# Computing the first W1 piece of batch 1 in the same array-mode group as batch 0's second piece

## The chip, the cores and the metric

One core of one Trainium2 chip. The metric is device time of one execution in microseconds (us); lower is better. Most executions agree within 0.3%, which is 0.6 us here, and the change is worth less than that, so much of this document is about how to see 0.2 us at all.

## The reference

Eight batches of cross attention between a sequence and a small state, both ways, then a two-layer block with silu over all the rows:

```python
scores = scale * x @ state.T ;  a  = softmax(scores)  ; xread = a  @ state   # (8, 8, 512, 64)
scores2 = scale * state @ x.T;  a2 = softmax(scores2) ; sread = a2 @ x       # (8, 8, 32, 64)
rows = concat([xread, sread], axis=2), heads joined                          # (4352, 512)
h = rows @ w_in                      # (., 2048)
out = (h * sigmoid(h)) @ w_out       # (., 512)
```

## The kernel before

The product `state @ w_in` is made once for each batch and called W1, so that `xread @ w_in` is `a @ W1`. W1 is 2048 columns wide and is made in pieces of 512. "G1 of tile k" is one 128-column tile of `a @ W1` (two matmuls) followed by silu on ScalarE; "G2 of tile k" is that tile's part of the last product (four matmuls for the four row groups of a batch).

A piece of W1 contracts over 64 and has 32 rows a head, so it uses the matmul array as eight tiles of 64x32. Eight matmuls, one a tile, make a piece into two PSUM banks. PSUM is the memory that the matmuls write their results to; a copy from there to the working memory (SBUF) is called an eviction below. The kernel uses eight PSUM banks: `psA` a0 to a3, `psH` two (tag h1), `psO` two.

```python
# cut: setup lines, returns and some arguments are left out; the whole kernel is below
def w1_mms(b, cols, new=bank):              # eight matmuls in 64x32 tiles
    for f, n in cols:
        for hg in range(2):
            pss[f, hg] = new([128, 512], FP32, "ps_w1")
        for s in range(4):
            for hg in range(2):
                nc.tensor.matmul(pss[f, hg][ds(32 * s, 32), 0:n], stT[ds(r, 64), b, ...],
                                 w_in_sb[ds(r, 64), h // 2, ds(f, n)], tile_position=(r, 32 * s), ...)
def w1_out(b, cols, engs, pss, at=0):       # PSUM to SBUF, one bank by VectorE, one by ScalarE
    ...
def g1_half(k, hg):
    if hg == 0:
        pool, tag = (psA, "a1") if k == 1 else (psH, "h1")
        h_ps[k] = pool.tile([128, 512], FP32, tag=tag, name="h1")
    nc.tensor.matmul(h_ps[k][:], W1[b][:, hg, ds(128 * ft, 128)], aT[b][:, hg, :, :], ...)

# loads on the GpSimd queue, in order (cut)
load_w_in(0, 128); load_w_in(128, 384); load_w_out(0, 2); load_w_out(2, 2)
# ... state of batch 1 ...
load_w_in(512)
load_w_out(4, 4)          # output weights of tiles 4 to 7, one transfer
# ... GpSimd's part of the first cast of x, normalisation ...
load_w_in(1024)
load_w_out(8, 4)

# batch 0
W0 = {2: (512, 512), 6: (1024, 512), 10: (1536, 512)}    # pieces of batch 0, by step
W1_AT = {4: 0, 6: 512}                                   # pieces of batch 1
LEAD0 = [2, 2, 2, 2, 2, 3, 2, 1, 3, 3, 2, 3]
for ft in range(12):
    upto(min(ft + LEAD0[ft], ready))                     # G1 of the next tiles
    if ft == 1:
        place_one_state(1, transpose_one_state(st1_n), nc.vector)
    if ft in W0:
        pss = w1_mms(0, [W0[ft]])
        if ft in W1_AT:
            pss1 = w1_mms(1, [(W1_AT[ft], 512)], new_h)  # rides in the same group
        w1_out(0, [W0[ft]], both, pss)
        if ft in W1_AT:
            w1_out(1, [(W1_AT[ft], 512)], both, pss1)
        ready = sum(W0[ft]) // 128
    elif ft in W1_AT:
        w1_cols(1, [(W1_AT[ft], 512)], both)             # a group of its own
    # ... G2 of tile ft ...
```

The softmax here doesn't subtract the row's maximum and nothing guards it: scores larger than these inputs give would overflow.

## Time and profile before

| | before |
|---|---|
| median of the first three runs | 213.09 us (213.04 to 213.17) |
| the profiled run | 214.55 us, span of the trace 212.8 us |
| matmul engine busy | 97% |
| ScalarE, VectorE, GpSimd busy | 65%, 35%, 19% |

The matmul groups of the page (line engine op, out<-in, shapes, count | busy us, mean ns of one | idle before; in these views PE is the matmul engine, PEld its weight loads, ACT is ScalarE, DVE VectorE and POOL GpSimd):

```profile
L563 PE MATMUL o<-w_out_sb,g 128*128 128x512 bf16 x481 | 129.5, 379 | 1.3 <-issue 0.5
L522 PE MATMUL h<-aT,W 128*128 128x512 bf16 x247 | 73.1, 379 | 0.2
L468 PE MATMUL ps_w<-w_in_sb,stT 64*32 64x512 bf16 (+2 forms) x264 | 10.2, 374 | 0.0
```

A matmul's 379 ns is its recorded length; they overlap and start 216 ns apart. The W1 groups (L468) are 264 of the 1550 matmuls recorded but only 10.2 us, since eight run together; what they cost beyond that are the holes at their edges.

### The profile page before, as it was taken

The page shows a single profiled execution, that of the slowest core. Times are in us where ns is not written, and L with a number is a line of the kernel's source. Part 1 is how long each engine was busy: PE and PEld are TensorE (multiplying, and loading weights), DVE is VectorE, ACT ScalarE, POOL GpSimd, SP SyncE. Part 2 cuts the span into 40 slices and gives each one's busy share as a digit, 9 for nine tenths or more (in the row PEclk, how much of TensorE's full clock was granted, in tenths as well). Part 3 has the DMA queues.
Part 4 walks back from the last instruction along what each step waited for, and adds up shares of the span by engine and source line. Part 5 has one row for each costly group of instructions (what it writes and reads, how often), then busy time and mean ns, then how long its engine had stood idle before and what let it go on. Part 6 is the DMA issues. An engine that isn't in the chain of part 4 may idle for free.

```text
span 212.8 us, 3839 instructions
## 1 busy us (share of the span) xinstructions
PE 205.8 (97%) x1550; PEld 97.9 (46%) x1575; DVE 73.8 (35%) x146; ACT 139.1 (65%) x244; POOL 39.9 (19%) x62
## 2 busy tenths in 40 slices
PE   7899999999999999999999999999999999999993
PEld 2543445345444434444444444444444444466653
DVE  2672246855851137104410752143512306100011
ACT  2685667899676877699469856886775256644410
POOL 8393213702420122012200302000200000000000
PEclk9999999999999999999999999999999999999998
DMA  5999999995639567464826429114230121011112
GB/s 189 192 205 207 285 261 313 249 242 203 99 78 265 174 130 170 101 195 102 218 64 211 79 53 240 49 52 99 65 83 17 64 82 52 0 49 49 52 49 99
DMA packets 42929, 28.65 MB, mean 135 GB/s; under 512 B 28064, under 2 KB 37792, under 8 KB 42912
## 3 DMA queue, kind: packets, MB, share of 16 engines
q1 hardware_dynamic: 36720, 20.65, 36.3%
q0 software_dynamic: 5904, 7.64, 17.4%
q8 instruction: 12, 0.20, 0.4%
q10 hardware_dynamic: 288, 0.13, 0.2%
q14 instruction: 5, 0.04, 0.1%
HBM read 17.43 MB, written 8.91 MB: 124 GB/s over the span
## 4 chain that ended last, share of the span: by engine, by line
PE 94%; DMA 2%; DVE 1%; issue 1%; ACT 0%
PE o L563 50%; PE h L522 26%; PE ps_w L468 4%; PE h L543 3%; PE o_a L563 3%; DMA x_f<-in_x_dram 2%; PE o_part L585 2%; PE ps_xt L252 1%; PE ps_sr L415 1%; PE ps_busy L165 1%; PE ps_sc L305 1%; PE ps_scT L331 1%; DVE W L159 1%; PE ps_at L397 0%; ACT xT L157 0%
## 5 line engine op out<-in xcount | busy, mean ns | idle before, releaser
L563 PE MATMUL o<-w_out_sb,g 128*128 128x512 bf16 x481 | 129.5, 379 | 1.3 <-issue 0.5
L554 ACT ACTIVATE g<-h 128x512 bf16<-128x512 f32 (+1 forms) x143 | 81.3, 573 | 35.3 <-PE h L522 20.6
L563 PEld LDWEIGHTS <-g 128*128 128x128 bf16 x528 | 50.2, 98 | 58.9 <-issue 3.8
L522 PE MATMUL h<-aT,W 128*128 128x512 bf16 x247 | 73.1, 379 | 0.2
L159 DVE COPY o_sb<-o 128x512 f32<-128x512 f32 x15 | 10.4, 690 | 91.9 <-PE o L563 87.3
L522 PEld LDWEIGHTS <-W 128*128 128x128 bf16 x254 | 24.4, 98 | 30.7 <-issue 1.2
L159 DVE CAST W<-ps_w 128x512 bf16<-128x512 f32 (+2 forms) x36 | 22.3, 658 | 23.8 <-PE ps_w L468 23.8
L157 ACT ACTIVATE W<-ps_w 128x512 bf16<-128x512 f32 (+1 forms) x32 | 16.3, 562 | 10.2 <-PE ps_w L468 10.2
L159 POOL CAST x_nat<-x_f 128x512 bf16<-128x512 f32 x24 | 14.6, 648 | 33.2 <-DMA x_f<-in_x_dram 33.2
L157 ACT ACTIVATE o_sb<-o 128x512 f32<-128x512 f32 x16 | 9.5, 597 | 14.3 <-PE o L563 11.8
L361 POOL TENSOR_TENSOR an<-e,rcn 128x512 bf16<-128x512 bf16 x5 | 7.6, 1517 | 49.1 <-DVE rcn L359 49.1
L468 PE MATMUL ps_w<-w_in_sb,stT 64*32 64x512 bf16 (+2 forms) x264 | 10.2, 374 | 0.0
L543 PE MATMUL h<-xmT,w_in_sb 128*128 128x256 bf16 x64 | 9.6, 273 | 0.1
L563 PE MATMUL o_a<-w_out_sb,g 128*128 128x512 bf16 x30 | 9.4, 379 | 0.1
L543 PEld LDWEIGHTS <-w_in_sb 128*128 128x128 bf16 x64 | 6.3, 98 | 3.9
L165 PE MATMUL ps_busy<-busy 128*128 128x512 bf16 x15 | 6.8, 563 | 1.2 <-DVE warm L172 1.2
L358 DVE TENSOR_REDUCE rs<-e 128x32 f32<-128x1024 bf16 x5 | 6.1, 1210 | 2.1 <-DMA e<-eT 2.1
L345 ACT ACTIVATE eT<-ps_scT 128x512 bf16<-128x512 f32 x10 | 5.4, 594 | 1.6 <-PE ps_scT L331 1.6
L784 ACT ACT_TABLE_LOAD x5 | 6.4, 1283 | 0.1
L381 POOL TENSOR_TENSOR an<-exp_nat,rc 128x512 bf16<-128x512 bf16 x3 | 3.1, 1046 | 17.7 <-ACT eT L345 10.8
L468 PEld LDWEIGHTS <-stT 64*32 64x32 bf16 x264 | 3.2, 90 | 5.5 <-issue 4.7
L109 POOL DMA_DIRECT2D x_f<-in_x_dram x4 | 3.3, 845 | 10.2 <-DVE x_rows L159 7.9
(76 smaller groups left out, 103.7 us busy)
## 6 DMA issues: line engine op xcount, KB each, us to landing
out_dram<-o_sb SPq DMA_DIRECT2D x33, 256.0 KB, 2.4
x_f<-in_x_dram SPq DMA_DIRECT2D x4, 1024.0 KB, 5.8
x_f<-in_x_dram POOLq DMA_DIRECT2D x2, 1024.0 KB, 11.1
w_in_sb<-in_moe_w_in_dram POOLq DMA_DIRECT2D x3, 512.0 KB, 10.1
x_f<-in_x_dram SPq DMA_DIRECT2D x2, 512.0 KB, 5.2
w_out_sb<-in_moe_w_out_dram POOLq DMA_DIRECT2D x4, 256.0 KB, 11.4
w_out_sb<-in_moe_w_out_dram POOLq DMA_DIRECT2D x2, 512.0 KB, 11.2
x_f<-in_x_dram POOLq DMA_DIRECT2D x2, 512.0 KB, 13.5
```

The lines of the kernel that those rows point to most:

```text
L157: nc.scalar.activation(dst, src, func=COPY, bias=0.0)
L159: eng.tensor_copy(dst, src)
L165: nc.tensor.matmul(ps[:], busy[:, 0:128], busy[:], start=True, stop=True, skip_group_check=True)
L345: nc.scalar.activation(t[:, hg], scT_ps[hg][:], func=EXP, bias=0.0, scale=SCALE)
L358: nc.vector.tensor_reduce(rs[:], e2[b][:], axis=AX, op=ADD)
L361: eng.tensor_tensor(a[:, hg], e2[b][:, hg], rc[:, hg].to_broadcast([128, 4, 4, NS]), op=MULT)
L468: nc.tensor.matmul(pss[f, hg][ds(32 * s, 32), 0:n], stT[ds(r, 64), b, h // 2, s % 2, :], w_in_sb[ds(r, 64), h // 2, ds(f, n)], start=True, ...
L522: nc.tensor.matmul(h_ps[k][:], W1[b][:, hg, ds(128 * ft, 128)], aT[b][:, hg, :, :], start=(hg == 0), stop=(hg == 1), skip_group_check=True,)
L543: nc.tensor.matmul(ps[:, 0:256], w_in_sb[:, kt, ds(128 * ft, 128)], xmT[:, :, kt].rearrange("p t n b -> p t (n b)"), start=(kt == 0), stop ...
L554: nc.scalar.activation(g[:, 0:n], ps[:, 0:n], func=SILU, bias=0.0)
L563: nc.tensor.matmul(outs[tt][:], gt[b * NFT + ft][:, ds(128 * tt, 128)], w_out_sb[:, ft, :], start=(ft == 0), stop=(ft == NFT - 1), skip_gr ...
L784: nc.scalar.activation(warm[:], busy[:, 0:1], func=SILU, bias=0.0)
```

## The change

Intent: each time the array changes between its full mode and the tiled one there is a hole in the stream of matmuls. Batch 0's second piece (step 2) and batch 1's first piece (step 4) were two groups. Now the latter rides in the group of step 2, in the two `psH` banks. Those banks must be free, so G1 of tile 3 goes one step earlier (`LEAD0[1]`), and while they are full G1 of tiles 4 and 5 goes to the two banks of batch 0's piece.

```diff
     def g1_half(k, hg):
         if hg == 0:
-            pool, tag = (psA, "a1") if k == 1 else (psH, "h1")
-            h_ps[k] = pool.tile([128, 512], FP32, tag=tag, name="h1")
+            if k == 1:
+                h_ps[k] = psA.tile([128, 512], FP32, tag="a1", name="h1")
+            else:
+                h_ps[k] = (bank if k in IN_BANKS else new_h)([128, 512], FP32, "h1")
...
+    IN_BANKS = (4, 5)
...
-    W1_AT = {4: 0, 6: 512}
-    LEAD0 = [2, 2, 2, 2, 2, 3, 2, 1, 3, 3, 2, 3]
+    W1_AT = {2: 0, 6: 512}
+    LEAD0 = [2, 3, 2, 2, 2, 3, 2, 1, 3, 3, 2, 3]
...
-        elif ft in W1_AT:
-            w1_cols(1, [(W1_AT[ft], 512)], both)
```

## The prediction

> **What bounds the kernel now.** I read the page first: busy shares, then the chain that ended last, then the instructions in order of time around the changed stage.
>
> ```profile
> PE 205.8 (97%) x1550; PEld 97.9 (46%) x1575; DVE 73.8 (35%) x146; ACT 139.1 (65%) x244; POOL 39.9 (19%) x62
> PEclk9999999999999999999999999999999999999998
> ...
> PE 94%; DMA 2%; DVE 1%; issue 1%; ACT 0%
> ```
>
> The matmul engine is busy for 97% of 212.8 us, its clock is never throttled, and it is 94% of the chain. No other engine is above 65%. So time comes off only if the stream of matmuls has fewer of them, or fewer gaps. The list of waits shows what gaps there are (engine and line <- releaser: us in total, times, longest):
>
> ```profile
> PEld L468 <- issue: 4.7, 12, 0.4
> PEld L563 <- issue: 3.8, 10, 0.4
> ```
>
> L468 is the W1 product, made of 64x32 tiles of the array; L563 is a full 128x128 product. Each of the twelve runs of L468 has a 0.4 us hole in the weight loads ahead of it, put down to no wait for another engine, and most have another behind. The changed stage in order of time (start, length, engine, line, tiles, count):
>
> ```profile
> 14.92 0.22 PE L206 MATMUL ps_st<-ident,st_n 128*128 128x128 bf16 x1
> 14.98 0.59 PE L563 MATMUL o<-w_out_sb,g 128*128 128x512 bf16 x2
> 15.41 0.81 PE L563 MATMUL o_a<-w_out_sb,g 128*128 128x512 bf16 x3
> 16.06 0.59 PE L522 MATMUL h<-aT,W 128*128 128x512 bf16 x2
> 16.58 0.41 PE L468 MATMUL ps_w<-w_in_sb,stT 64*32 64x512 bf16 x8
> 16.92 0.39 PE L563 MATMUL o<-w_out_sb,g 128*128 128x512 bf16 x1
> ...
> 19.11 0.59 PE L522 MATMUL h<-aT,W 128*128 128x512 bf16 x2
> 19.63 0.11 PEld L468 LDWEIGHTS <-stT 64*32 64x32 bf16 x8 [0.42 <-issue]
> 19.97 0.55 PEld L563 LDWEIGHTS <-g 128*128 128x128 bf16 x4 [0.23 <-issue]
> ...
> 22.14 0.59 PE L563 MATMUL o_a<-w_out_sb,g 128*128 128x512 bf16 x2
> 22.67 0.63 PE L468 MATMUL ps_w<-w_in_sb,stT 64*32 64x512 bf16 x16
> 23.23 0.60 PE L563 MATMUL o<-w_out_sb,g 128*128 128x512 bf16 x2
> ```
>
> A group of 8 at 16.58 (second piece of batch 0), another of 8 at 19.64 (first piece of batch 1), a group of 16 at 22.67 (a piece of each). The change makes the first two one group of 16, at the place of the first. The rest of the span repeats what the third shows.
>
> **What the Trainium skill says.** "TensorEngine Tiling (Array Packing)", Key Properties: "Changing tiling mode (not just tile) drains the TensorE". The trace agrees in effect: full-array matmuls follow one another at 0.216 us (15.409, 15.625, 15.840 by the recorded starts), but the group starts 0.309 after the matmul before it (16.272 to 16.581), and the next full one 0.318 after the group's last start (16.605 to 16.923).
> "TensorE: Matmul & The Clock Gate", The mechanism: different tiles run together, about 4 ns apart. Here the eight starts run from 16.581 to 16.605, 3.4 ns apart, and the second eight of the group of 16 begin 0.203 us after the last of the first eight (22.694 to 22.897). So a set of eight costs about one full matmul.
> "PSUM — Partial Sum Buffer", PSUM bank collisions: the semaphores must guard whole banks. That is why the riding piece needs banks of its own, and why the two G1 results must go elsewhere. No collision is in question here.
>
> **The change part by part.** The order of instructions of the changed kernel against the old one on each engine (built, not run) shows equal counts on every engine, no change of order on VectorE, GpSimd and the DMA queue, one ScalarE eviction moved two places up, and the matmul order restored after G1 of tile 5. So nothing is computed less; only one mode switch in and one out go away.
>
> *Group of 8.* From the last full matmul before it to the second after it (the second, because the first after a group has its weights loaded late): 16.272 to 17.150 = 0.878. Two ordinary steps of 0.216 are 0.432. Cost: 0.446.
> *Group of 16.* 22.361 to 23.454 = 1.093, less 0.432: 0.661.
> *Merging.* 2 x 0.446 - 0.661 = **0.231 us** saved, all on the matmul stream, hence on the path.
>
> *A small wait that vanishes.* G1 of tile 4 needs the piece evicted by VectorE: 17.055 + 0.692 = 17.747, weights load at 17.800, its matmuls at 17.805 and 18.030. Without a wait its second would be at 17.365 + 3 x 0.216 = 18.013 (one output matmul at about 17.58 is missing from the records; the order has four). Gain **0.017**, if the new order has no such wait: see the next two items.
>
> *G1 of tile 3 goes ahead of the small transpose of batch 1's state.* Its two matmuls (0.432) go before the transpose, which moves from 14.921 to about 15.353. VectorE's four placing copies, 15.178 to 16.137, then end at about 16.569. The merged group wants its second weight load at 16.583, and this load waits for VectorE (the bank of the transpose is reused). The lag from a VectorE end to a weight load was 0.053 above, so it can go at 16.622. **Cost 0.04.** In the old order this had 0.4 us to spare.
>
> *Banks of the riding piece.* They held G1 of tiles 2 and 3. Tile 2's activation runs at 15.121 to 15.72 as before; tile 3's matmuls now end at about 15.137 + 0.379 = 15.52, so its activation follows at about 15.61 and ends at 16.21. The riding half wants the banks at 16.62 + 0.23 = 16.85. No wait; 0.6 us spare.
>
> *G1 of tile 4.* Group at 16.62 in effect, output matmuls at 17.18, 17.41, 17.62, 17.84, so G1 at 18.06, with its weights wanted at 17.84. VectorE's eviction begins 0.45 after the last of the first eight (17.055 against 16.605), in the group of 16 also (23.144 against 22.694): 16.645 + 0.45 + 0.69 + 0.05 = 17.84. Just met. ScalarE is earlier than before, because tile 3's activation no longer stands ahead of its eviction. Banks: tile 4 and tile 5 take the two banks of batch 0's piece, evicted by about 17.8, which G1 of tile 4 waits for in any case.
>
> *G2 of tile 4* wants its activation when its weights load at about 19.57: G1 ends at 18.27 + 0.38, activation from 18.69 to 19.29. Met, and ScalarE has lost the eviction that stood here.
>
> *Sum.* 0.231 + 0.017 - 0.04 = 0.208. Following the starts through by hand, G1 of tile 6 moves from 20.850 to 20.645, which is 0.205: the same but for rounding.
>
> **Does the gain reach the end?** The absolute clock here is the load queue, which is full in this stage (206 GB/s from 13.4 to 16.6 us). By the landings in the trace: weights of the second W1 piece land at 15.13, wanted at 16.58; output weights of tiles 4 to 7 at 17.64, wanted at 19.78; the third W1 piece's at 20.21, wanted at 22.46; the fourth's at 25.32, wanted at 27.65; batch 1's x at 28.27, its second half wanted at about 29.3. A shift of 0.2 uses none of these margins up. After 24 us the matmul engine's waits on others are 0.6 us for activations, 0.6 for a W eviction and 0.2 for GpSimd, all on work that hangs on the matmul stream itself and moves with it. So I take the gain through whole: 213.09 - 0.21 = **212.88 us**.
>
> **The rivals.**
> *A new wait eats it.* Placing the state copies (the 0.04 above) or the eviction for G1 of tile 4, met with nothing to spare. If VectorE is 0.1 later than I think, both grow by 0.1: saving near 0.1, time near 213.0. For it: two margins of zero. Against it: the lengths are those of the same instructions in this trace.
> *Later absorption.* If a transfer fixed in time is the next to be met, the PE waits 0.2 longer there and the end is at 213.1. Against it: the margins listed, the smallest about 1.0 us.
> *The reorder costs beyond the model.* Tile 4's, 5's and 6's G1 now carry a wait on the matmul engine's own semaphore, as their banks were last written in the other mode. If each broke the pipelining as a switch does (0.1 each), 0.3 would be lost and the time be 213.2. Against it: the first output matmul, at 13.842, carries such a wait in the old order and starts 0.216 after the one before.
> *More than a switch.* If the freed ScalarE slot near 20 us mattered, 0.05 more could come: 212.8. But no matmul in this stage waits for ScalarE there.
>
> **Range and chances.** The three timed runs before span 0.13 us, so the gain is barely above that spread, and chip-to-chip differences may add some. The rivals put the time from 212.8 to 213.2; I take 212.65 to 213.1 for 8 in 10, since the losses need a mechanism that the trace doesn't show. Two per cent would be 4.3 us, twenty times the sum: 0.99 for within 2%, the rest split.
>
> **What would show it right or wrong.** Right: eleven holes at L468 in place of twelve, total near 4.3; a run of 16 at about 16.6 and none near 19.6; the second load of that group 0.03 to 0.06 after the first; G1 of tile 6 at about 20.65; everything after 21 us earlier by an even 0.2. Wrong: a hole ahead of the G1 pair near 18.06 or between the halves of the group; a PE wait later on that grew by what was saved here; or a group of 16 that costs over 0.75.

## The result, and the profile after

| | before | changed |
|---|---|---|
| median | 213.06 us (212.81 to 213.17, 4 runs) | 212.92 us (212.85 to 213.54, 4 runs) |
| ratio of the fast runs | | 1.0001 (0.9981 to 1.0022) |
| span of the profiled run | 212.8 us | 211.8 us |

Ratios here are the mean time of one kernel's fast runs over that of the other's of the same rounds, so not quite the ratio of the medians quoted. One run of the changed kernel, the profiled one at 213.54, lifts the mean; the other three are 212.85 to 212.93. The predicted 212.88 is 0.04 from the median, but the interval is 0.9 us wide, over four times the effect, so the time alone confirms nothing but "within 2%". That the median came within 0.04 of the forecast is luck.

The changed stage in the first profile of the changed kernel, in order of time (start, length, engine, line, tiles, count [idle before <- what ended it]; L565 and L524 are the old L563 and L522):

```profile
15.27 0.25 PEld L468 LDWEIGHTS <-stT 64*32 64x32 bf16 x16 [0.42 <-issue]
15.38 0.63 PE L468 MATMUL ps_w<-w_in_sb,stT 64*32 64x512 bf16 x16
...
18.11 0.59 PE L524 MATMUL h<-aT,W 128*128 128x512 bf16 x2
18.32 0.10 PEld L565 LDWEIGHTS <-g 128*128 128x128 bf16 x1
18.74 0.60 ACT L556 ACTIVATE g<-h 128x512 bf16<-128x512 f32 x1 [0.70 <-PE h L524]
19.00 0.59 PE L565 MATMUL o<-w_out_sb,g 128*128 128x512 bf16 x2 [0.29 <-DMA w_out_sb<-in_moe_w_out_dram]
```

The group of 16 is there, but so are two things that the prediction had ruled out. The group's matmuls start 0.416 us after the last full one (14.964 to 15.380 by the recorded starts) in place of 0.309: the second piece's weights landed at 15.34. And the first G2 matmul of tile 4, whose weights were loaded at 18.32, starts at 19.00, 0.673 after the matmul before it in place of 0.216: the output weights of tiles 4 to 7 landed at 18.95. In the profile of before they landed at 17.64.

So this profile lost 0.107 + 0.457 us to the load queue and still was 1 us shorter than the first. Comparing every silu of the two traces shows where that came from: G1 of tile 1 is already 1.31 us earlier, ahead of anything the change touches; tile 6 is 0.99 earlier, and from there every activation is 0.99 to 1.00 earlier, up to the end. About half a microsecond of it is x, whose first cast begins at 5.01 us in place of 5.51; the rest comes up between there and tile 1, and goes with the array's clock, which was up sooner, as the length of single matmuls tells. The same eight transposes of x, before and then changed (lines of the two timelines):

```profile
6.12 1.03 PE L252 MATMUL ps_xt<-ident,x_rows 128*128 128x128 bf16 x8 [0.44 <-DVE x_rows L159]
```

```profile
5.50 0.86 PE L252 MATMUL ps_xt<-ident,x_rows 128*128 128x128 bf16 x8
```

One transpose took 314 ns nearly throughout the first of these; in the second it fell from 314 to 219 within the eight. (The page's clock row says 9 in every slice but the last one before, and doesn't show this. The prediction's "its clock is never throttled" was read from that row, and is wrong for the start.) "TensorE: Matmul & The Clock Gate", What's actually happening, says that the array starts at half clock and gets the full one after about 3.4 us of activity, at a moment that differs between runs. The traces agree that it differs: in one profile (e1) a matmul at 4.45 us is already short (390 ns), in the first profile the transposes at 9.04 still take 314. They don't bear out 3.4 us in each case: matmuls run from 1.19 us on in both, with idle stretches, so the full clock came within 3.3 us in e1 and after more than 7.8 in the first profile. Where it came later, so did tile 1's silu: the first short matmuls are at 4.09 us in e4 and at 7.20 in e11, the silus at 12.43 and 12.69. The x load and the clock together moved the start by over a microsecond.

**How the traces are compared from here.** The span divides into three: the start, up to tile 1's silu; the changed stage, from tile 1's silu to tile 6's; and the rest. The rest took 191.26 to 191.30 us in all thirteen profiles. So the change has no effect after tile 6 that is larger than 0.04, and the stage can be measured to about 0.01 us while the time itself scatters by several tenths. In the table below, "waits" are what a gap in the starts exceeds the same gap in a profile without a wait for a landing (0.309 into a group, 0.216 between full matmuls, 0.318 out of a group).

| run | tile 1's silu at | stage | wait, W1 weights | wait, output weights | stage less waits | output weights landed |
|---|---|---|---|---|---|---|
| before | 14.042 | 7.440 | 0 | 0 | 7.440 | 17.64 |
| changed | 12.734 | 7.754 | 0.107 | 0.457 | 7.190 | 18.95 |
| e1 (before again) | 12.494 | 7.552 | 0.118 | 0 | 7.434 | 18.50 |
| e2 (changed again) | 12.563 | 7.288 | 0 | 0.064 | 7.224 | 18.32 |
| e3 (group split) | 12.509 | 7.459 | 0 | 0 | 7.459 | 17.14 |
| e4 (lead alone) | 12.425 | 7.470 | 0 | 0 | 7.470 | 18.04 |
| e5 (changed, two loads) | 12.994 | 7.228 | 0 | 0 | 7.228 | 15.63 (tiles 4, 5) |
| e6 (before, two loads) | 12.957 | 7.439 | 0 | 0 | 7.439 | 15.96 (tiles 4, 5) |
| e7 (changed, late load) | 12.545 | 9.631 | 0 | 2.406 | 7.225 | 20.64 |
| e8 (before, late load) | 12.648 | 9.040 | 0 | 1.619 | 7.421 | 20.15 |
| e9 (changed, half later) | 12.642 | 7.228 | 0 | 0 | 7.228 | 16.02 (tiles 4, 5) |
| e10 (before, half later) | 12.611 | 7.440 | 0 | 0 | 7.440 | 16.31 (tiles 4, 5) |
| e11 (e9, transpose first) | 12.692 | 7.191 | 0 | 0 | 7.191 | 16.24 (tiles 4, 5) |

The first profile of the changed kernel stands at 7.190 and not at 7.22 because its wait for the W1 weights covers another of 0.035, for the placing copies (e11 below): its first eight starts of the group span 0.024 us, those of e2 0.058.

### The profile page after: what moved, and what is told of

Its sections match the earlier page's. It is cut to its first block, busy times and chain, and to the rows that moved or that the text cites. A ratio compares the mean times of both kernels' runs of the same rounds, so it can differ in the third digit from the quotient of the medians.

```text
span 211.8 us, 3839 instructions
## 1 busy us (share of the span) xinstructions
PE 204.5 (97%) x1550; PEld 97.1 (46%) x1575; DVE 73.6 (35%) x146; ACT 139.4 (66%) x244; POOL 40.0 (19%) x62
## 4 chain that ended last, share of the span: by engine, by line
PE 88%; DMA 6%; POOL 2%; issue 1%; DVE 0%; POOLq 0%
PE o L565 50%; PE h L524 25%; DMA w_out_sb<-in_moe_w_out_dram 6%; PE ps_w L468 3%; PE h L545 3%; PE o_a L565 2%; PE o_part L587 2%; PE ps_sr L415 1%; POOL w_in_sb L150 1%; PE ps_scT L331 1%; POOL w_out_sb L153 1%; PE ps_sc L305 0%; PE ps_xt L252 0%; DVE W L159 0%; POOL st_n L190 0%
## 5 line engine op out<-in xcount | busy, mean ns | idle before, releaser
L565 PE MATMUL o<-w_out_sb,g 128*128 128x512 bf16 x480 | 129.3, 379 | 1.6 <-issue 0.5
L565 PEld LDWEIGHTS <-g 128*128 128x128 bf16 x528 | 50.3, 98 | 59.5 <-issue 4.4
L524 PE MATMUL h<-aT,W 128*128 128x512 bf16 x247 | 73.0, 379 | 0.1
L524 PEld LDWEIGHTS <-W 128*128 128x128 bf16 x254 | 24.5, 98 | 30.5 <-issue 1.2
L565 PE MATMUL o_a<-w_out_sb,g 128*128 128x512 bf16 x31 | 9.8, 379 | 0.2
L165 PE MATMUL ps_busy<-busy 128*128 128x512 bf16 x15 | 6.3, 530 | 1.2 <-DVE warm L172 1.2
```

The costliest lines, as they stand in the source:

```text
L165: nc.tensor.matmul(ps[:], busy[:, 0:128], busy[:], start=True, stop=True, skip_group_check=True)
L565: nc.tensor.matmul(outs[tt][:], gt[b * NFT + ft][:, ds(128 * tt, 128)], w_out_sb[:, ft, :], start=(ft == 0), stop=(ft == NFT - 1), skip_gr ...
```

## The experiments

The theory: the merge saves one pair of mode switches, about 0.21 us of the stage, and what reaches the end is that less what a late landing takes back. Rivals: the landing sets the time anyway, so nothing is saved; or the gain comes from the early G1 or the banks. All runs were correct. e1 to e4 shared a chip, e5 to e8 another, e9 to e11 a third; times are compared within a chip.

**e1_before: the kernel before, unchanged.**

> The kernel before, unchanged, against itself: the noise floor, and a second look at its start. Both theories: ratio 1.000, within 0.0005 or so. In the trace: two groups of 8, each costing 0.44 to 0.45 us over ordinary matmuls. Switch theory (the merge saves one pair of mode switches, 0.23 us, and it reaches the end): if the array's clock is up early, as in the profile of the changed kernel (start 1.3 us earlier), the output product of tile 4 starts near 18.67 us, and if the weights of tiles 4 to 7 land later than that it waits here too. Absorption theory (the landing of these weights sets the time in ordinary runs, so the merge only lengthens a wait): the wait is there, with the landing at about 18.9.

Measured: 213.15 us against 213.12 (11 runs, 212.82 to 213.77), ratio 0.9999 (0.9984 to 1.0014). With five rounds the noise floor is thus 0.3 us, more than the effect. In the trace the clock was up early, tile 1's silu 1.5 us earlier than in the first profile:

```profile
14.51 0.59 PE L522 MATMUL h<-aT,W 128*128 128x512 bf16 x2
15.15 0.41 PE L468 MATMUL ps_w<-w_in_sb,stT 64*32 64x512 bf16 x8
...
17.67 0.59 PE L522 MATMUL h<-aT,W 128*128 128x512 bf16 x2
18.20 0.41 PE L468 MATMUL ps_w<-w_in_sb,stT 64*32 64x512 bf16 x8
18.54 0.60 PE L563 MATMUL o<-w_out_sb,g 128*128 128x512 bf16 x2
```

The first group waits 0.118 for its weights. The output product of tile 4 starts at 18.541, the weights landed at 18.50: just in time. So the margin of over 2 us that the first profile showed had two causes: the output product of tile 4 came 1.43 us later there (19.976), and the weights landed 0.86 us earlier (17.64).

**e2_after: the changed kernel again.**

> The changed kernel again, with five rounds, since the first comparison (ratio 1.0001, 0.9981 to 1.0022) can't tell 0.2 us from nothing. Switch theory: 0.15 to 0.25 us faster than before, ratio 0.9988 to 0.9993. Absorption theory: within 0.05 us of before, and the trace has a wait for the output weights of tile 4 (0.457 us of lost time in the first profile).

Measured: 213.08 us (212.90 to 213.39), ratio 0.9995 (0.9980 to 1.0010): a difference of medians of 0.04, between the two theories and inside the noise. The trace decides more:

```profile
14.36 0.81 PE L565 MATMUL o_a<-w_out_sb,g 128*128 128x512 bf16 x3
15.10 0.66 PE L468 MATMUL ps_w<-w_in_sb,stT 64*32 64x512 bf16 x16
15.70 0.60 PE L565 MATMUL o<-w_out_sb,g 128*128 128x512 bf16 x2
...
17.86 0.59 PE L524 MATMUL h<-aT,W 128*128 128x512 bf16 x2
18.36 0.59 PE L565 MATMUL o<-w_out_sb,g 128*128 128x512 bf16 x2
```

A group of 16 with no wait ahead of it (14.793 to 15.102), and a gap of 0.280 in place of 0.216 ahead of tile 4's G2 (18.079 to 18.359): the weights landed at 18.32, so 0.064 was given back. The holes ahead of the W1 groups are eleven, as predicted, against the twelve of before; one is now put down to the landing of W1 weights (list of waits):

```profile
PEld L468 <- issue: 3.8, 10, 0.4
PEld L468 <- DMA w_in_sb<-in_moe_w_in_dram: 0.4, 1, 0.4
```

The stage less waits is 7.224, against 7.440 and 7.434 for the kernel before.

**e3_split: one full matmul between the two halves of the group.**

```diff
             if ft in W1_AT:
+                if ft == 2:
+                    G2(0, 0, ft)
                 pss1 = w1_mms(1, [(W1_AT[ft], 512)], new_h)
...
-        for tt in range(3):
+        for tt in range(ft == 2, 3):
             G2(0, tt, ft)
```

> The changed kernel with one output matmul of tile 2 between the two halves of the merged group, which brings the second pair of mode switches back; banks, leads and all other order stay as changed. Switch theory: 0.2 us slower than the changed kernel, so equal to before within 0.05; the two half groups cost 0.44 each, 0.88 to 0.90 together against 0.66. Absorption theory: equal to the changed kernel within 0.05, the wait for the output weights shorter by 0.2. A third theory, that the gain is from G1 of tile 3 being early or from the banks: equal to the changed kernel, without any such wait.

Measured: 213.38 us (213.01 to 214.59, 6 runs), ratio 1.0022 (0.9997 to 1.0047); two runs of six near 214.5 make this. The trace has no wait for a landing:

```profile
14.31 0.81 PE L565 MATMUL o_a<-w_out_sb,g 128*128 128x512 bf16 x3
15.05 0.45 PE L468 MATMUL ps_w<-w_in_sb,stT 64*32 64x512 bf16 x8
15.43 0.39 PE L565 MATMUL o<-w_out_sb,g 128*128 128x512 bf16 x1
15.75 0.41 PE L468 MATMUL ps_w<-w_in_sb,stT 64*32 64x512 bf16 x8
16.09 0.39 PE L565 MATMUL o<-w_out_sb,g 128*128 128x512 bf16 x1
```

From the last full matmul before (14.739) to the second after (16.314) are 1.575 us; three ordinary steps are 0.648, so the two halves cost 0.927. The same reckoning for e2's group (14.793 to 15.921, two steps) gives 0.696. The difference, 0.231, is the mode switch, and so is the stage's: 7.459 against 7.228 of e9. Banks, leads and evictions were those of the changed kernel, so the third theory falls.

**e4_lead: the early G1 of tile 3 alone.**

```diff
-    LEAD0 = [2, 2, 2, 2, 2, 3, 2, 1, 3, 3, 2, 3]      # kernel before
+    LEAD0 = [2, 3, 2, 2, 2, 3, 2, 1, 3, 3, 2, 3]
```

> The kernel before with G1 of tile 3 one step earlier (ahead of the small transpose of batch 1's state), and nothing else: this part of the change alone. Switch theory as predicted: 0.00 to 0.04 us slower than before, from the second weight load of the first group waiting 0.04 for the placing copies. Absorption theory: equal to before. Third theory (the early G1 is what helps): 0.1 us or more faster.

Measured: 213.36 us (213.00 to 214.61), ratio 1.0027 (1.0000 to 1.0053), again with two runs near 214.5 that were not traced. (Their spans, and those of e3's two, are 212.7 and 212.8 us, like that of the first profile with its late start; that they too started late is not shown.) The stage took 7.470, 0.03 more than before, as expected, and the first eight matmuls of the first group start over 0.059 us in place of 0.024. In the stage this part of the change alone costs, it doesn't gain.

**e5_after_two_loads and e6_before_two_loads: the output weights in two transfers.** The same edit to either kernel:

```diff
     load_w_in(512)
-    load_w_out(4, 4)
+    load_w_out(4, 2)
+    load_w_out(6, 2)
```

> The changed kernel with the output weights of tiles 4 to 7 loaded as two transfers of two tiles instead of one of four, so that tiles 4 and 5 land some 0.65 us earlier. Switch plus landing theory (the merge saves 0.21 us of matmul time, of which a late landing of these weights takes a part back in runs that start early): no wait before the output product of tile 4; from the activation of tile 2 to that of tile 6 takes 6.11 to 6.16 us (6.361 in the first profile of before, 6.209 with a wait of 0.064 in the second profile of the changed kernel); 0.2 to 0.3 us faster than before, ratio 0.9985 to 0.9991. Pure switch theory (the landings don't matter): the same as the changed kernel, 0.05 to 0.1 faster than before, as the second comparison had it.

> The kernel before with the same two transfers. Switch plus landing theory: that stage takes 6.36 us plus at most the 0.12 that the second W1 piece's weights cost in one profile; before seldom waits for the output weights, so 0.0 to 0.1 us faster than before, and e5 is faster than this one by 0.15 to 0.25. Rival: splitting helps both equally, e5 and e6 apart by no more than 0.1.

| | e5 (changed) | e6 (before) | the unaltered kernel before |
|---|---|---|---|
| all runs | 213.21 to 213.28 (6) | 213.43 to 213.58 (6) | 212.80 to 214.50 (11) |
| median | 213.26 | 213.45 | 213.11 |
| ratio to before | 1.0000 (0.9977 to 1.0024) | 1.0011 (0.9990 to 1.0032) | |

Two findings. The difference of e5 and e6 is 0.19 us, with no overlap of the runs: the saving, for once visible in the times. Neither trace has a wait for a landing, and the runs of each scatter little (0.07 and 0.15). The stages differ by 0.211 (7.439 and 7.228). But the expectation that both would be faster than before was missed: they start 0.4 to 0.6 us later than e1 to e4. The GpSimd lines of e5's timeline show a reason, which e9 and e10 test below:

```profile
5.02 0.84 POOL L150 DMA_DIRECT2D w_in_sb<-in_moe_w_in_dram  x1
5.85 1.42 POOL L153 DMA_DIRECT2D w_out_sb<-in_moe_w_out_dram  x2
7.25 0.44 POOL L159 CAST x_rows<-x_f 128x256 bf16<-128x256 f32 x1
```

GpSimd issues these loads itself, some 0.7 us each, and its share of the first cast of x comes after them: at 7.25 in place of 6.51 in e2. That this also made the start so regular is plausible, as the cast then is later than whatever the clock or the x load delays; it was not tested.

**e7_after_late and e8_before_late: the suspected wait made large.** In either kernel:

```diff
     load_w_in(512)
-    load_w_out(4, 4)
+    load_w_in(1024)
...
-    load_w_in(1024)
+    load_w_out(4, 4)
     load_w_out(8, 4)
```

> The suspected wait doubled: the changed kernel with the output weights of tiles 4 to 7 loaded after the third W1 piece's weights, so that they land at about 20.2 to 21.5 us, 2 us or more after they are wanted (18.3). Landing theory: the output product of tile 4 starts 0.04 after the landing, the kernel is 1.5 to 3 us slower than before, and the merge's 0.2 us are gone: equal to e8 but for the landing's own spread (0.3 us or so). If the merge saved time in another way than by reaching this point sooner, e7 stays 0.2 faster than e8.

> The kernel before with the same late load. Landing theory: as slow as e7 (1.5 to 3 us slower than before), with the wait ahead of the output product of tile 4 shorter by about 0.2 than in e7 when the landing is at the same time. Rival: 0.2 us slower than e7.

Measured: e7 215.07 us (214.53 to 216.82), ratio 1.0095 (1.0062 to 1.0128); e8 214.81 (214.51 to 215.27), ratio 1.0076 (1.0051 to 1.0101). The wait in e7 and then in e8:

```profile
18.06 0.10 PEld L565 LDWEIGHTS <-g 128*128 128x128 bf16 x1
...
20.68 0.59 PE L565 MATMUL o<-w_out_sb,g 128*128 128x512 bf16 x2 [2.24 <-DMA w_out_sb<-in_moe_w_out_dram]
```

```profile
18.24 0.41 PE L468 MATMUL ps_w<-w_in_sb,stT 64*32 64x512 bf16 x8
20.20 0.59 PE L563 MATMUL o<-w_out_sb,g 128*128 128x512 bf16 x2 [1.55 <-DMA w_out_sb<-in_moe_w_out_dram]
```

Both start about 0.045 after the landing (20.64 and 20.15). e7 waited 0.787 longer: 0.49 for its later landing, 0.10 for its earlier start, and the remaining 0.19 is the merge's saving, turned wholly into waiting. With the landing as the bound the merge buys nothing; e7 is not 0.2 faster than e8. By the median it is even the slower, but the two intervals overlap, and it is the traces that decide.

**e9_after_half_later and e10_before_half_later: two transfers, the second issued after the cast.** In either kernel:

```diff
     load_w_in(512)
-    load_w_out(4, 4)
+    load_w_out(4, 2)
...
+    load_w_out(6, 2)
     load_w_in(1024)
```

> Two loads again, but the second (tiles 6 and 7) issued just ahead of the third W1 piece's weights, so that GpSimd's part of the first cast of x is no longer behind a further issue of 0.7 us (the cast began at 7.25 us in e5, at 6.51 in the second profile of the changed kernel, and the start was 0.4 later). Landing theory: no wait for the output weights, activation of tile 1 at 12.4 to 12.7 us, tile 2 to tile 6 in 6.11 to 6.16 us or up to 0.12 more if the second W1 piece's weights land late; 0.15 to 0.35 us faster than before, 0.1 faster than the changed kernel. If the landing cost nothing in ordinary runs: equal to the changed kernel (second comparison, 213.08) within 0.05.

> The kernel before with the same loads. Switch theory: 0.2 us slower than e9 (0.15 to 0.25), as e6 against e5 (213.45 against 213.26); about equal to before or up to 0.1 faster. Rival (the gap between e5 and e6 came from their starts): no difference to e9 beyond 0.1.

Measured: e9 212.68 us (212.64 to 212.91), ratio 0.9989 (0.9977 to 1.0001); e10 213.09 (212.76 to 213.30), ratio 1.0001 (0.9989 to 1.0013); before 212.95 (212.80 to 213.28, 11 runs). GpSimd's part of the cast begins at 6.47 and 6.45 again and the starts are back (12.64 and 12.61), which bears out the reason given under e5 and e6. No landing is waited for, and the stages differ by 0.212. The medians differ by 0.41, more than expected; five runs each with spreads of 0.27 and 0.54 can't carry the excess. e9 has the lowest median of the versions that were run, 0.27 below before's on its chip, but its interval still touches 1, and by the 2% measure it is the same.

**e11_place_first: e9 with the small transpose ahead of G1 of tiles 2 and 3.**

```diff
-        upto(min(ft + LEAD0[ft], ready))
         if ft == 1:
             place_one_state(1, transpose_one_state(st1_n), nc.vector)
+        upto(min(ft + LEAD0[ft], ready))
```

> e9 with the small transpose of batch 1's state back ahead of G1 of tiles 2 and 3, so that the placing copies end before the merged group wants its second weight load. If the 0.04 of the prediction is a wait for these copies: the group's first eight starts span 0.024 us in place of 0.059, and tile 2 to tile 6 take about 6.17 us, but counted from a tile 2 that starts 0.06 later; 0.03 to 0.04 us faster than e9 up to tile 6, too little for the timed runs. If it comes from the mode switch itself: the same 0.059.

Measured: 212.92 us (212.53 to 213.28), ratio 0.9995 (0.9982 to 1.0008). In the trace the first eight starts span 0.023 in place of 0.058, the group from its first start to the next full matmul takes 0.558 in place of 0.593, and the stage is 7.191, 0.037 shorter than e9's. So the predicted 0.04 is a wait for the placing copies (the four VectorE copies that put batch 1's transposed state in place), and it can be had back by order alone. The copies tell the same: in e9 the last ends at 15.164 and the group's second weight load starts 0.053 later, the lag that the prediction took; in e11 they end at 14.348. The times can't show it.

## Why the prediction was right or wrong

- **The bound.** Right: everything after tile 6 takes 191.26 to 191.30 us in each trace, whatever the change did before it, so the matmul stream carries the time and a saving there is kept.
- **Merging, 0.231.** Right: e3, which brings one pair of switches back, costs 0.231 more. Two groups of 8 and one of 16 in the same trace were enough to price it.
- **The small wait at G1 of tile 4, 0.017.** Gone, as predicted; in e2 no gap before G1 of tile 4 exceeds the ordinary one, so the eviction that was to be "just met" was met.
- **The placing copies, 0.04.** Right at 0.035 to 0.037 (e4, e11).
- **Sum for the stage, 0.208.** The changed kernel's stage was 0.212 shorter where no landing interfered (e10 against e9), 0.211 for e6 against e5.
- **The rivals.** The extra waits on the matmul engine's own semaphore cost nothing that the starts show. VectorE was on time. "Later absorption" was dismissed too easily.
- **"Does the gain reach the end?"** This is the step that failed. I read the margins of the loads from the one profile and called the smallest 1.0 us; for the output weights it showed 19.78 - 17.64 = 2.1. But compute's start and the load queue are two clocks, and in that run both widened the margin. Its compute had started 1.3 to 1.6 us later than in every other profile with the same order of loads ahead of the cast, and the landing itself ranged from 17.14 to 18.95. In an early run of the changed kernel the weights are wanted at about 18.3, so the margin is from +1.2 to -0.6. Measured, the changed kernel waited 0.457 for them in one profile and 0.064 in the other. Of the 0.457, 0.21 is the merge's saving, given back whole; the other 0.25 the kernel before would have waited too with that start and that landing (worked out, not run). So the matmul stream lost its 0.21, but the gain did not always come through whole. The warning stood in the table: the profiled run was 1.46 us over the median.
- **The time.** 212.92 and, on another chip, 213.08, with differences of 0.14 and 0.04 of the medians from before, where 0.21 was predicted. The medians have the predicted sign; the means of the first comparison don't (ratio 1.0001). A part returned to the load queue would explain a gain under 0.21, but the noise floor of 0.3 us doesn't let the times prove either number. How much is given back in the mean of all runs stays open; two profiles of the changed kernel are too few.

Also open: why the landing spreads so. In the worst profile fifteen of the sixteen parts of that transfer had landed by 17.73 and the last by 18.95; in the best (e3) all sixteen by 17.14.

## What to carry to other kernels

Count the switches of the array's mode, price a pair from two groups of different size in the same trace (0.23 us here), and put small tiled products into a group that is there anyway, if banks can be found. Before you call a load hidden, ask how the profile's start compares with the other runs: a margin is the difference of two clocks, and a late start makes every load look early. And when an effect is smaller than the scatter of the times, measure the stage between two fixed instructions in each trace, and make one experiment in which the suspected wait can't occur and one in which it must.

## What the Trainium skill lacked or had wrong

- "TensorEngine Tiling (Array Packing)", Key Properties, says that a change of tiling mode drains the engine, but not what that costs. Here: 0.309 us from the last full matmul to the first tiled one and 0.318 from its last start to the next full one, where an ordinary step is 0.216; a pair costs 0.231 with the late weight load after it (e3 against e9).
- "TensorE: Matmul & The Clock Gate", Part 1, gives the moment of the full clock a spread of 500 ns either way under sustained matmuls. The kernel here isn't that case, as its start waits for input in between; the clock came before 4.45 us in one profile and after 9.04 in another; tile 1's silu was 1.5 us apart between these two, of which about 0.4 was the landing of x.
- "DMA: Bandwidth & Descriptors", Why a DMA increments its semaphore by 16 and not by 1, says that only all sixteen increments mean landed. The runs agree and add a size: the last increment of one 512 KB load came 0.07 (e8) to 1.22 us (first profile of the changed kernel) after the fifteenth, and in both profiles of the changed kernel as it stood this last part alone made the matmuls wait.
- No page that I read has a figure for how long GpSimd is held by the issue of one such load (latency to the first byte, which is given, is another thing): 0.7 to 0.9 us each here (e5), which delayed a cast that stood behind it.
